# Attention into channel mix on one core: batch 0 loaded in fewer, larger pieces, and each later batch's loads held behind the crossbar transpose of the batch ahead

## The chip, the cores and the metric

The kernel runs on one NeuronCore of a Trainium2 chip. The metric is device time in microseconds (us), from start to end of one execution; the median of several executions counts. The engines are TensorE (PE; its weight loads are listed as PEld), VectorE (DVE), ScalarE (ACT), GpSimd (POOL) and SyncE (SP). Each engine takes its instructions in the order of its own list. POOL and SP issue the transfers here, and 16 DMA engines move the data.

## The reference

Two stages, for 8 batches of 576 tokens with 8 heads of 64:

```python
kv  = einsum('bhsd,bhse->bhde', k, v)          # 64x64 for each batch and head
o   = einsum('bhsd,bhde->bhse', q, kv)
x   = o / sqrt(mean(o*o, -1) + 1e-6) * g_norm  # heads side by side: (8, 576, 512)
xp  = x shifted by one token, zero in front
xk  = mu_k*x + (1-mu_k)*xp;   xr = mu_r*x + (1-mu_r)*xp
kk  = relu(xk @ w_k)                           # w_k 512x1024
out = sigmoid(xr @ w_r) * ((kk*kk) @ w_v)      # w_r 512x512, w_v 1024x512
```

q, k, v, the weights and the output are float32 in memory; the kernel turns inputs into bfloat16 while it loads them.

## The kernel before

**Attention, by batch.** `load(b, n, h0, h1)` (L253) has POOL issue one transfer that brings heads h0 to h1 of q, k or v of batch b, 96 tokens of 6 consecutive positions on 96 partitions. Batch 0 comes in twelve transfers of two heads, batch 1 in six of four, batches 2 to 7 in three of eight heads each (`whole`, L305). The tags k, v and q have two buffers each, so a load of batch b+2 must also wait until batch b's buffer has been read. For a batch: `kv` (L496) multiplies k and v on PE, `kvc` copies the result out; q is turned so that head_dim lies on partitions; `u` (L575) multiplies the turned q, `qT`, with kv; `uc` copies that out, `sq` squares it, `ss` (L597) sums the squares by a matmul with a block of ones, `rr` takes the reciprocal root on ACT, `mul` scales, `d` takes the difference to the token before, and `xk`, `xr` blend.

**How q is turned.** Batches 0 to 2 turn q on PE with an identity (`qtr`, L356 and L553) and copy it out of PSUM (`qc`). Batches 3 to 7 (`BY_DMA`) first regroup the loaded q into a buffer q2 by copies on DVE or ACT (`ql`, L517), and then SP issues one transposing transfer from q2 to qT (`qt`, L531). q2 has one buffer, qT two.

**The gate.** After `qt` of batch b, for b = 3, 4, 5, POOL copies one element of qT (`gate`, L538). POOL cannot run that copy before the transpose has landed, so all that stands behind it in POOL's list is held; the loads of batch b+2 are declared to stand behind it.

**Channel mix, by groups of 512 tokens.** `mix(g)` for nine groups: `k{g}.0` to `.7` (L689, 8 times 4 matmuls of 512 columns), `relu` on ACT, `ksq` (square) on DVE, `r{g}.0` to `.3` (L741, 16 matmuls) with `sig` on ACT, `v{g}.c.p` (L763, 32 matmuls), `out` (product with the sigmoid, on DVE) and `store` on SP. Group 0's k part is cut into `k0.a` (L452, by head pair) and `k0.b` (L709). Both halves of w_k are first multiplied by g_norm on DVE (`g.w_k0`, `g.w_k1`, L289).

**What sets the order.** A table of tokens, `ORDER` (L15 to L63): `Planner.run` goes through it and emits the pieces as they stand there, so it sets the order within each engine's list; the part behind a colon picks the engine, `#2` is the second piece of that name, and `idle:n` puts n matmuls on zeros (L659) into PE's list. Waits between engines are added by the framework from the tiles that are read and written.

Of the kernel before, what the change touches and what calls it, by code (L numbers as in the profile page):

```python
# [15 lines left out]
setup table loadq0.2 loadq0.4 loadv0.4 ident idle:23 qtr0.2 small qtr0.1 loadk0.4 qc0.1#2:DVE loadk0.6 loadq0.6
qc0.1:ACT qc0.2:ACT idle:2 kv0.2 kvc0.2#2:DVE kvc0.2:DVE idle:4 u0.2 loadv0.6 uc0.2:DVE qc0.2#2:ACT sq0.2 idle:3
qtr0.3 qc0.3:DVE idle:4 kv0.3 kvc0.3:ACT kvc0.3#2:ACT qc0.3#2:DVE edge ident9 idle:6 u0.3 u0.2#2 uc0.3:DVE sq0.3
loadv0.0 ss0.2 loadq0.0 rr0.2 idle:8 ss0.3 rr0.3 uc0.2#2:DVE sq0.2#2 mul0.2 loadk0.2 loadv0.2 idle:7 kv0.1
kvc0.1#2:ACT qtr0.0 loadk0.0 qc0.0#2:DVE idle:2 kv0.0 tr9 kvc0.1:DVE qc0.0:DVE u0.1 kvc0.0#2:DVE d0.2 mul0.3 d0.3  # L20
cols ss0.2#2 kvc0.0:ACT u0.0 uc0.1:ACT mk0.2:DVE uc0.0:ACT mk0.3:ACT idle:7 u0.0#2 rr0.2#2 sq0.1 w_k1 idle:4 ss0.1
xk0.2 xk0.3 sq0.0 mul0.2#2 uc0.0#2:ACT sq0.0#2 g.w_k1 idle:4 ss0.0 idle:16 k0.a1.2 d0.2#2 rr0.0 w_k0 rr0.1 mul0.1
loadq1.4 mul0.0 d0.0 mr0.3:DVE d0.1 g.w_k0 loadq1.0 k0.a1.3 ss0.0#2 idle:19 k0.a0.3 rr0.0#2 mr0.1:DVE k0.a0.2
mk0.1:ACT xk0.1 k0.a0.1 qtr1.2 mk0.0:DVE xr0.3 xk0.0 mul0.0#2 d0.0#2 mk0.1#2:DVE mk0.2#2:ACT mk0.0#2:DVE mk0.3#2:ACT
mr0.0:ACT mr0.1#2:DVE loadk1.0 k0.a1.1 xk0.2#2 qc1.2:ACT xk0.0#2 loadv1.0 k0.a1.0 relu0.01 w_r mr0.2:ACT xr0.2
k0.a0.0 relu0.00 qtr1.0 kv1.0 k0.b0 loadk1.4 kvc1.0:ACT mr0.2#2:ACT mr0.0#2:ACT xr0.0 qc1.0:DVE xr0.1 ksq0.01 u1.01
uc1.01:ACT loadv1.4 relu0.10 k0.b1 relu0.11 mr0.3#2:DVE u1.00 g.w_r:DVE xr0.0#2 xr0.2#2 r0.0 uc1.00:DVE w_v r0.1
sig0.0 ksq0.00 ksq0.11 kv1.2 kvc1.2:DVE sq1.00 u1.10 uc1.10:DVE loadv2.0 u1.11 ksq0.10 r0.2 uc1.11:ACT sq1.11 ss1.00
rr1.00 r0.3 sq1.01 ss1.01 v0.0.0 rr1.01 sig0.1 ss1.11 loadk2.0 rr1.11 v0.0.1 sq1.10 ss1.10 rr1.10 v0.1.0 v0.1.1
loadq2.0 v0.2.0 v0.2.1 v0.3.0 v0.3.1 mul1.0 d1.0 xk1.0 loadq3.0 out0.0 mul1.2 d1.2 kv2.0 kvc2.0:ACT qtr2.0 qc2.0:ACT  # L30
qtr2.2 xk1.2 out0.1 k1.0 k1.1 qc2.2:DVE xr1.0 u2.11 ql3.2:DVE uc2.11:ACT relu1.0 ql3.3:DVE ql3.1:DVE ql3.0:ACT u2.00
uc2.00:DVE sq2.00 k1.2 k1.3 k1.4 loadv3.0 relu1.1 k1.5 ksq1.0 u2.10 loadk3.0 relu1.2 xr1.2 u2.01 ksq1.2 uc2.10:ACT
sq2.10 uc2.01:ACT loadq4.0 sq2.01 store0.0#2 k1.6 k1.7 relu1.3 ksq1.3 ss2.00 rr2.00 r1.0 sq2.11 ss2.01 qt3 rr2.01
loadv4.0 r1.1 ksq1.1 r1.2 r1.3 kv3.0 mul2.0 sig1.0 d2.0 ss2.10 sig1.1 kvc3.0:DVE xk2.0 v1.0.0 store0.0 rr2.10 ss2.11
rr2.11 xr2.0 ql4.2:ACT v1.0.1 ql4.3:ACT v1.1.0 mul2.2 loadk4.0 v1.1.1 out1.0 v1.2.0 ql4.0:ACT ql4.1:DVE u3.11 u3.01
v1.2.1 v1.3.0 uc3.01:ACT d2.2 uc3.11:ACT u3.10 uc3.10:ACT xk2.2 u3.00 uc3.00:ACT v1.3.1 k2.0 k2.1 relu2.0 sq3.10
ss3.10 store0.1#2 gate3 loadq5.0 out1.1 k2.2 rr3.10 sq3.01 k2.3 sq3.11 ss3.11 rr3.11 ss3.01 sq3.00 rr3.01 relu2.1
ksq2.0 k2.4 kv4.0 ss3.00 rr3.00 k2.5 relu2.2 xr2.2 mul3.2 kvc4.0:DVE qt4 u4.10 ql5.1:DVE ql5.0:DVE uc4.10:DVE sq4.10
u4.01 store1.0#2 ksq2.2 mul3.0 k2.6 k2.7 ql5.2:DVE uc4.01:ACT store0.1 ql5.3:ACT relu2.3 ksq2.3 u4.00 uc4.00:ACT
u4.11 r2.0 r2.1 uc4.11:ACT d3.2 loadv5.0 sig2.0 ksq2.1 store1.0 sq4.01 ss4.10 rr4.10 r2.2 r2.3 loadk5.0 d3.0 kv5.0  # L40
xk3.2 kvc5.0:DVE v2.0.0 sq4.00 sq4.11 qt5 xr3.0 v2.0.1 v2.1.0 v2.1.1 xk3.0 out2.0 ss4.00 sig2.1 ss4.01 v2.2.0 rr4.00
rr4.01 store2.0 mul4.0 gate4 loadk6.0 store1.1 v2.2.1 v2.3.0 u5.00 uc5.00:DVE u5.10 v2.3.1 out2.1 xr3.2 k3.0 k3.1
d4.0 relu3.0 uc5.10:ACT ksq3.0 ss4.11 sq5.10 store2.0#2 k3.2 loadq6.0 ql6.0:DVE k3.3 rr4.11 store1.1#2 relu3.1
ksq3.1 k3.4 k3.5 gate5 mul4.2 u5.11 relu3.2 ksq3.2 xk4.0 ql6.2:ACT u5.01 uc5.11:ACT sq5.00 k3.6 k3.7 ql6.1:ACT r3.0
sq5.11 relu3.3 r3.1 uc5.01:DVE loadv6.0 sig3.0 ql6.3:ACT d4.2 ksq3.3 xr4.2 kv6.0 kvc6.0:DVE xr4.0 r3.2 r3.3 loadq7.0
store2.1 ss5.11 v3.0.0 qt6 sq5.01 v3.0.1 v3.1.0 v3.1.1 sig3.1 rr5.11 ss5.01 v3.2.0 v3.2.1 xk4.2 ss5.00 rr5.00 rr5.01
v3.3.0 out3.0 v3.3.1 store3.0#2 k4.0 k4.1 relu4.0 ss5.10 out3.1 ql7.2:ACT store3.1#2 mul5.0 ql7.1:DVE rr5.10 d5.0
xk5.0 xr5.0 k4.2 ksq4.0 store2.1#2 k4.3 relu4.1 k4.4 ql7.0:ACT k4.5 relu4.2 u6.10 ksq4.1 u6.00 store3.0 ksq4.2
ql7.3:ACT uc6.10:ACT qt7 uc6.00:DVE sq6.00 k4.6 k4.7 relu4.3 sq6.10 ksq4.3 r4.0 r4.1 u6.11 uc6.11:DVE u6.01 r4.2
store3.1 r4.3 uc6.01:DVE sig4.0 ss6.10 mul5.2 ss6.00 sig4.1 v4.0.0 v4.0.1 loadk7.0 d5.2 xk5.2 rr6.10 rr6.00 v4.1.0  # L50
# [794 lines left out]
```

## Time and profile before

| | |
|---|---|
| median of 3 runs | 220.46 us (220.01 to 221.04) |
| profiled execution: time | 220.13 us |
| profiled execution: span from first to last instruction | 218.4 us |
| PE busy | 198.6 us (91%) |
| DVE busy | 147.1 us (67%) |
| ACT busy | 127.9 us (59%) |
| POOL busy | 30.3 us (14%) |
| moved by DMA | 29.43 MB, 16.78 MB of it by the transfers that POOL issues (queue q0), nearly all the rest by those of SP (q1) |
| granted PE clock, mean | 0.984 |

Busy time is the sum of an engine's instructions; PE's includes the matmuls on zeros. An engine that is busy a small share of the span can still hold up another one at one place, so the waits and the timeline tell more than the shares. "Releaser" is what an instruction waited for last, as the profile infers it.

### The profile page before, as it was taken

To read this page: it belongs to the slowest core of one execution; us is meant where nothing else is said; L and a number is where in the kernel's file an instruction comes from. 1 tells how busy PE (TensorE), PEld (TensorE's weight loads), DVE (VectorE), ACT (ScalarE), POOL (GpSimd) and SP (SyncE) were. 2 spreads that over 40 slices of the span, in tenths; PEclk is the share of its full clock that TensorE was granted. 3 is DMA by queue.
4 is the path that set the end of the run, shared out by engine and by line. 5 is a ranking of instruction groups with operands and counts; after the bars stand their busy time and mean duration, and the time that the engine had idled before them with its cause. 6 is when DMAs were issued, how large, how long until landed. Compare 5 with 4: busy or idle time off the path is not lost.

```text
span 218.4 us, 4018 instructions
## 1 busy us (share of the span) xinstructions
PE 198.6 (91%) x1596; PEld 104.9 (48%) x1615; DVE 147.1 (67%) x319; ACT 127.9 (59%) x162; POOL 30.3 (14%) x48
## 2 busy tenths in 40 slices
PE   5698999999983982999999999999999999999992
...
DMA  4999999999998999995999537250024005115015
GB/s 66 155 199 203 205 207 203 203 225 203 156 191 158 165 155 258 148 144 110 228 238 201 140 100 156 48 144 3 0 63 133 0 0 164 34 26 138 28 33 159
DMA packets 39271, 29.43 MB, mean 135 GB/s; under 512 B 13516, under 2 KB 34772, under 8 KB 39252
## 3 DMA queue, kind: packets, MB, share of 16 engines
q0 software_dynamic: 21632, 16.78, 51.8%
...
## 4 chain that ended last, share of the span: by engine, by line
PE 62%; DMA 32%; POOL 2%; issue 1%; DVE 0%; DVEq 0%; POOLq 0%
PE mm L689 22%; PE mm L763 20%; DMA qT<-q 14%; DMA q<-in_q_dram 12%; PE mm L741 11%; DMA k<-in_k_dram 5%; PE at L597 2%; PE at L575 2%; PE at L780 2%; PE mm L780 2%; PE at L496 1%; POOL q L255 1%; PE at L553 1%; POOL k L255 1%; POOL w_k L281 0%
## 5 line engine op out<-in xcount | busy, mean ns | idle before, releaser
L689 PE MATMUL mm<-xk,w_k 128*128 128x512 bf16 (+1 forms) x282 | 59.8, 362 | 0.3
L763 PE MATMUL mm<-w_v,sqk 128*128 128x512 bf16 x250 | 59.5, 387 | 0.3
L693 ACT ACTIVATE relu<-mm 128x1024 bf16<-128x1024 f32 x36 | 36.9, 1025 | 35.1 <-PE mm L689 23.5
L689 PEld LDWEIGHTS <-w_k 128*128 128x128 bf16 x288 | 28.0, 99 | 26.7 <-issue 2.8
L763 PEld LDWEIGHTS <-sqk 128*128 128x128 bf16 x256 | 24.9, 99 | 29.1 <-issue 3.2
L741 PE MATMUL mm<-w_r,xr 128*128 128x512 bf16 x137 | 33.4, 379 | 0.4
L696 DVE TENSOR_TENSOR sqk<-relu 128x1024 bf16<-128x1024 bf16 x32 | 21.7, 688 | 15.7 <-ACT relu L693 15.7
L767 DVE TENSOR_TENSOR out<-mm,sig 128x1024 f32<-128x1024 f32 x16 | 19.5, 1221 | 14.8 <-PE mm L763 7.1
L601 ACT ACTIVATE rs<-at,eps 128x576 bf16<-128x576 f32 x28 | 19.9, 739 | 8.0 <-PE at L597 7.2
L190 ACT ACT_TABLE_LOAD x18 | 23.1, 1283 | 1.0 <-PEq L829 0.7
L741 PEld LDWEIGHTS <-xr 128*128 128x128 bf16 x144 | 13.6, 98 | 15.5 <-issue 0.7
L746 ACT ACTIVATE sig<-mm 128x1024 bf16<-128x1024 f32 x18 | 18.3, 1024 | 3.3 <-PE mm L741 3.1
L639 DVE TENSOR_SCALAR md<-d,cols 128x576 bf16<-128x576 bf16 x56 | 18.2, 368 | 0.3
L181 ACT CAST uT<-at 128x576 bf16<-128x576 f32 x18 | 11.0, 640 | 10.0 <-PE at L575 9.9
L575 PE MATMUL at<-qT,kv 64*64 64x288 bf16 x112 | 6.5, 299 | 9.0 <-DMA qT<-q 8.6
L582 DVE TENSOR_TENSOR sq<-uT 128x576 bf16<-128x576 bf16 x28 | 11.9, 452 | 3.5 <-ACT uT L181 3.4
L613 DVE TENSOR_TENSOR xT<-uT,rs 128x1152 bf16<-128x1152 bf16 x14 | 10.5, 753 | 3.2 <-ACT rs L601 3.2
L181 ACT COPY q<-q 96x384 bf16<-96x384 bf16 (+1 forms) x16 | 9.4, 628 | 5.6 <-DMA qT<-q 5.6
L659 PE MATMUL mm<-zero 128*128 128x128 bf16 x109 | 11.0, 260 | 1.1 <-DVE zero L227 1.1
L597 PE MATMUL at<-sq,ones 128*128 128x288 bf16 x56 | 11.0, 287 | 0.1
L642 DVE TENSOR_TENSOR xr<-md,xT 128x1152 bf16<-128x1152 bf16 x14 | 10.6, 759 | 0.5
L642 DVE TENSOR_TENSOR xk<-md,xT 128x1152 bf16<-128x1152 bf16 x14 | 10.6, 759 | 0.5
...
## 6 DMA issues: line engine op xcount, KB each, us to landing
...
v<-in_v_dram POOLq DMA_DIRECT2D x6, 576.0 KB, 16.7
k<-in_k_dram POOLq DMA_DIRECT2D x6, 576.0 KB, 17.1
q<-in_q_dram POOLq DMA_DIRECT2D x6, 576.0 KB, 13.0
...
```

The source lines that it names most:

```text
L181: nc.scalar.copy(out=dst, in_=src)
L190: nc.scalar.preload_act_table_set(name)
L601: nc.scalar.activation(out=get(rs)[:, hs, cs], in_=ps.t[:, :, 0:HS], func=AF.Abs_reciprocal_sqrt, bias=eps, scale=1.0 / HD)
L639: nc.vector.tensor_scalar(out=get(md)[:, hp], in0=d.t[:, hp], scalar1=cols[:, m0 + hp:m0 + hp + 1], scalar2=None, op0=ALU.mult)
L642: nc.vector.tensor_tensor(out=dst[:, hs, c0:c0 + S], in0=md.t[:, hs], in1=xT.t[:, hs, 0:S], op=ALU.add)
L689: nc.tensor.matmul(get(ps)[:, fc % 2, a0:a1], w_k_sb[:, cc, 128 * fc:128 * fc + 128], xk[:, cc, x0:x0 + a1 - a0], start=(cc == 0), stop=(c ...
L693: nc.scalar.activation(out=get(rt), in_=ps.t, func=AF.Relu)
L696: nc.vector.tensor_mul(out=get(sqk)[:, 2 * f2:2 * f2 + 2, :], in0=rt.t, in1=rt.t)
L741: nc.tensor.matmul(get(ps)[:, ci % 2, :], xr[:, cc, n0:n0 + 128], w_r_sb[:, cc, :], start=(cc == 0), stop=(cc == NHP - 1))
L746: nc.scalar.activation(out=get(sg), in_=ps.t, func=AF.Sigmoid)
L763: nc.tensor.matmul(get(ps)[:, ci % 2, :], sqk.t[:, fc, 128 * ci:128 * ci + 128], w_v_sb[:, fc, :], start=(fc == 0), stop=(fc == NFC - 1))
L767: nc.vector.tensor_mul(out=get(ot)[:, xs, :], in0=ps.t[:, xs, :], in1=sg.t[:, xs, :])
```

## The change

The loop that loads batch 0 takes pieces of four, two and two heads instead of four times two: nine transfers instead of twelve. The gate behind the transpose of batch b now holds the loads of batch b+1 instead of b+2, and stands behind the transposes of batches 3 to 6 instead of 3 to 5. So the loads of batch 4 are held for the first time, and those of batches 5 to 7 are held by a transpose that comes one batch later. `ORDER` is a new table: head pair 0 is taken first instead of pair 2, and all pieces up to the end stand in a new order. Two lines stand for the table here.

```diff
 ORDER = """
-setup table loadq0.2 loadq0.4 loadv0.4 ident idle:23 qtr0.2 small qtr0.1 loadk0.4 qc0.1#2:DVE loadk0.6 loadq0.6
+setup table loadk0.0 ident loadq0.0 idle:31 qtr0.0 loadv0.0 ident9 idle:6 kv0.0 loadq0.4 loadv0.4 kv0.1 qc0.0#2:ACT
...
-        p = add({"POOL": 0.64 if b == 0 else 0.76}, fn, bufs=[kvq[(n, b)]], due=due, land=(h1 - h0) * (0.42 if b == 0 else 0.37),
+        p = add({"POOL": 0.64 if b == 0 else 0.76}, fn, bufs=[kvq[(n, b)]], due=due, land=(h1 - h0) * (0.39 if b == 0 else 0.37),
...
-    for hp in range(NHP):
+    for h0, h1 in ((0, 4), (4, 6), (6, 8)):
         for i, n in enumerate(("k", "v", "q")):
-            load(0, n, 2 * hp, 2 * hp + 2, -900 + 10 * hp + i)
+            load(0, n, h0, h1, -900 + 10 * h0 + i)
...
-            if b + 2 < B:
+            if b + 1 < B:
                 gate = add({"POOL": 0.3}, lambda _: nc.gpsimd.tensor_copy(out=turned, in_=qT.t[0:1, 0, 0:1]), deps=[c],
                            bufs=[qT], name=f"gate{b}")
                 for n in ("k", "v", "q"):
-                    whole[(n, b + 2)].deps.append(gate)
+                    whole[(n, b + 1)].deps.append(gate)
```

The numbers 0.39 and 0.42 (`land`) are read by nothing that runs: `Planner.add` drops them.

How the lists move, at three places. First, POOL's list from batch 0's loads to the two halves of w_k; a name such as `q_91` is a tile with its number, `96x2x384` is two heads, `x2` two such instructions in a row, and the waits on DMASW are on an earlier transfer of POOL. Before:

```order
L255 DMA q_91<-in_q_dram 96x2x384 x2
L255 DMA v_94<-in_v_dram 96x2x384
L238 AFFINE_SELECT ident_69<-ident_69 128x128 [waits DVE_49]
L255 DMA k_153<-in_k_dram 96x2x384 x2
L255 DMA q_91<-in_q_dram 96x2x384
L255 DMA v_94<-in_v_dram 96x2x384 x2
L255 DMA q_91<-in_q_dram 96x2x384 [waits DMASW0_49]
L255 DMA k_153<-in_k_dram 96x2x384 [waits DMASW1_49]
L255 DMA v_94<-in_v_dram 96x2x384 [waits DMASW2_49]
L255 DMA k_153<-in_k_dram 96x2x384 [waits DMASW3_49]
L281 DMA w_k_79<-in_moe_w_k_dram 128x4x512 [waits DMASW4_49]
L281 DMA w_k_79<-in_moe_w_k_dram 128x4x512 [waits DMASW5_49]
```

After:

```order
L255 DMA k_91<-in_k_dram 96x4x384
L238 AFFINE_SELECT ident_69<-ident_69 128x128 [waits DVE_49]
L255 DMA q_96<-in_q_dram 96x4x384
L255 DMA v_143<-in_v_dram 96x4x384
L255 DMA q_96<-in_q_dram 96x2x384
L255 DMA v_143<-in_v_dram 96x2x384
L255 DMA k_91<-in_k_dram 96x2x384 x2
L255 DMA v_143<-in_v_dram 96x2x384
L255 DMA q_96<-in_q_dram 96x2x384 [waits DMASW0_49]
L281 DMA w_k_79<-in_moe_w_k_dram 128x4x512 [waits DMASW1_49]
L281 DMA w_k_79<-in_moe_w_k_dram 128x4x512 [waits DMASW2_49]
```

Heads 0 to 3 of k, q and v now come first, in three transfers of four heads; what follows w_k up to the load of q of batch 3 keeps its order.

Second, POOL's list from the last loads of batch 3 on; `turned` is the gate. Before:

```order
L255 DMA v_944<-in_v_dram 96x8x384 [waits DMASW4_49,DMASW2_49,PE_49]
L255 DMA k_959<-in_k_dram 96x8x384 [waits DMASW3_49]
L255 DMA q_975<-in_q_dram 96x8x384 [waits DMASW0_49,PE_49]
L255 DMA v_1009<-in_v_dram 96x8x384 [waits DMASW6_49,DMASW5_49]
L255 DMA k_1125<-in_k_dram 96x8x384 [waits DMASW7_49]
L538 COPY turned_77<-qT_1006 1x1 [waits DMAHW6_49]
L255 DMA q_1201<-in_q_dram 96x8x384 [waits DMASW1_49,DVE_49,Activation_49]
```

After:

```order
L255 DMA v_857<-in_v_dram 96x8x384 [waits DMASW7_49,DMASW1_49,PE_49]
L255 DMA k_937<-in_k_dram 96x8x384 [waits DMASW0_49]
L538 COPY turned_77<-qT_946 1x1 [waits DMAHW0_49]
L255 DMA q_954<-in_q_dram 96x8x384 [waits DMASW5_49,PE_49]
L255 DMA k_1128<-in_k_dram 96x8x384 [waits DMASW4_49,DMASW2_49]
L255 DMA v_1184<-in_v_dram 96x8x384 [waits DMASW3_49]
L538 COPY turned_77<-qT_1202 1x1 [waits DMAHW7_49,Pool_49]
```

The three loads of batch 4, which stood ahead of the first gate, now stand behind it, and a second gate stands between them and the loads of batch 5.

Third, DVE's list around the regrouping of batch 3's q (`q2<-q`), behind group 0's last output. Before:

```order
L767 TENSOR_TENSOR out_890<-mm_750,sig_722 128x1024 [waits PE_49]
L183 COPY qT_860<-at_862 128x1152 [waits PE_49]
L639 TENSOR_SCALAR md_902<-d_771,cols_72 128x576 x2
L642 TENSOR_TENSOR xr_82<-md_902,xT_767 128x2x576 [waits DVE_49]
L183 COPY q2_911<-q_777 96x2x6x64 [waits DMASW1_49]
L183 COPY q2_911<-q_777 96x6x64 x4
L183 CAST uT_913<-at_922 128x2x288 [waits PE_49]
```

After:

```order
L767 TENSOR_TENSOR out_781<-mm_764,sig_723 128x1024 [waits PE_49]
L183 COPY qT_861<-at_832 128x1152 [waits PE_49]
L183 COPY q2_889<-q_711 96x6x64 [waits DMASW6_49]
L183 COPY q2_889<-q_711 96x6x64 x3
L183 COPY q2_889<-q_711 96x2x6x64
L183 CAST uT_909<-at_904 128x2x288 [waits PE_49]
L582 TENSOR_TENSOR sq_911<-uT_909 128x2x288 [waits DVE_49]
L639 TENSOR_SCALAR md_930<-d_747,cols_72 128x576 x2
L642 TENSOR_TENSOR xr_82<-md_930,xT_743 128x2x576 [waits DVE_49]
```

The regrouping, which waits for the load of q of batch 3, moved ahead of the blend `xr`, and the last of its copies (not shown) came behind that blend.

## Rows read from the trace of the kernel before

**Rows 1.** The page's 40 slices of the span: busy tenths of PE and of DMA.
```profile
PE   5698999999983982999999999999999999999992
...
DMA  4999999999998999995999537250024005115015
```
**Rows 2.** Waits of PE from 44 to 140 us: us in total, times, longest.
```profile
PE at L575 <- DMA qT<-q: 8.6, 2, 4.6
```
**Rows 3.** Timeline of PE: start, us, operation, count, idle before and its releaser.
```profile
68.82 0.55 PE L575 MATMUL at<-qT,kv 64*64 64x288 bf16 x8 [4.06 <-DMA qT<-q]
69.30 3.43 PE L763 MATMUL mm<-w_v,sqk 128*128 128x512 bf16 x8
...
73.90 1.89 PE L689 MATMUL mm<-xk,w_k 128*128 128x512 bf16 x7
...
85.77 0.44 PE L575 MATMUL at<-qT,kv 64*64 64x288 bf16 x8 [4.56 <-DMA qT<-q]
86.14 3.54 PE L689 MATMUL mm<-xk,w_k 128*128 128x512 bf16 x8
```
**Rows 4.** Windows: busy PE, PEld, DVE, ACT, POOL, then granted PE clock, DMA share, GB/s.
```profile
69.00:73.00 4.00, 4.00 (x24) 1.19 (x16) 2.37 (x6) 3.33 (x6) 2.43 (x4) 0.57 0.61 86
...
86.00:90.00 4.00, 4.00 (x25) 1.20 (x18) 3.25 (x8) 1.74 (x4) 1.56 (x3) 0.57 0.79 145
```
**Rows 5.** SP's timeline: the first of the five transposes being issued.
```profile
51.49 8.78 SPq L532 DMA_TRANSPOSE qT<-q  x1
```
**Rows 6.** Transposes issued in 51:60, in 115:119 and in 130:134: count, us to landing.
```profile
qT<-q SPq DMA_TRANSPOSE x1, 17.3
...
qT<-q SPq DMA_TRANSPOSE x1, 6.3
...
qT<-q SPq DMA_TRANSPOSE x1, 4.9
```
**Rows 7.** DMA queues in 60:62, then in 132:134: packets, MB, share of 16 engines.
```profile
q0 software_dynamic: 376, 0.28, 90.6%
q1 hardware_dynamic: 373, 0.10, 36.1%
...
q1 hardware_dynamic: 1628, 0.42, 109.9%
```
**Rows 8.** POOL's timeline: loads of batches 3 (two), 4 and 5.
```profile
27.54 0.77 POOL L255 DMA_DIRECT2D q<-in_q_dram  x1 [1.65 <-PE at L553]
...
35.21 0.77 POOL L255 DMA_DIRECT2D k<-in_k_dram  x1
47.37 0.77 POOL L255 DMA_DIRECT2D q<-in_q_dram  x1 [11.39 <-PE at L553]
...
69.36 0.77 POOL L255 DMA_DIRECT2D q<-in_q_dram  x1 [0.36 <-issue]
```
**Rows 9.** Loads issued in 27:28, 35.1:36, 69:70 and 100:100.5: KB, us to landing.
```profile
q<-in_q_dram POOLq DMA_DIRECT2D x1, 576.0 KB, 21.9
...
k<-in_k_dram POOLq DMA_DIRECT2D x1, 576.0 KB, 20.1
...
q<-in_q_dram POOLq DMA_DIRECT2D x1, 576.0 KB, 6.4
...
v<-in_v_dram POOLq DMA_DIRECT2D x1, 576.0 KB, 9.1
```
**Rows 10.** Windows of 5 us at the start, columns as in rows 4.
```profile
5.00:10.00 5.00, 3.39 (x46) 2.24 (x46) 1.13 (x4) 1.08 (x3) 4.66 (x8) 1.00 1.13 145
10.00:15.00 5.00, 4.46 (x53) 3.62 (x54) 2.67 (x10) 1.12 (x4) 4.27 (x7) 1.00 1.26 192
15.00:20.00 5.00, 4.45 (x79) 3.37 (x76) 4.50 (x21) 3.50 (x9) 1.63 (x3) 1.00 1.25 206
```
**Rows 11.** The chain that ended last: start, us, what.
```profile
25.06 20.74 DMA q<-in_q_dram
```
**Rows 12.** Window 90:135, columns as in rows 4.
```profile
90.00:135.00 45.00, 44.79 (x359) 24.35 (x360) 39.45 (x79) 36.09 (x44) 3.25 (x5) 1.00 0.96 169
```

More of the change, by code (lines that the diff above doesn't have):

```diff
@@ L15 @@
 ORDER = """
[L16 to L50, printed above, removed]
@@ L61 @@
-k8.0 k8.1 relu8.0 ksq8.0 k8.2 store7.0#2 k8.3 relu8.1 k8.4 ksq8.1 k8.5 relu8.2 k8.6 k8.7 relu8.3 ksq8.2 r8.0 r8.1
-sig8.0 ksq8.3 r8.2 r8.3 v8.0.0 v8.0.1 out8.0 v8.1.0 v8.1.1 sig8.1 v8.2.0 out8.0#2 v8.2.1 v8.3.0 out8.1 store8.0#2
-v8.3.1 v8.3.0#2 store8.0 v8.3.1#2 store8.1 out8.1#2 store8.1#2 out8.1#3 store8.1#3
+setup table loadk0.0 ident loadq0.0 idle:31 qtr0.0 loadv0.0 ident9 idle:6 kv0.0 loadq0.4 loadv0.4 kv0.1 qc0.0#2:ACT
+kvc0.1:ACT kvc0.1#2:ACT kvc0.0:ACT loadk0.6 loadk0.4 qc0.0:DVE qtr0.1 qc0.1#2:DVE kvc0.0#2:ACT idle:5 u0.0#2
@@ new lines @@
+uc0.0#2:DVE qc0.1:ACT idle:1 u0.1 uc0.1:DVE u0.0 uc0.0:ACT qtr0.2 sq0.1 idle:7 kv0.2 kvc0.2:ACT qc0.2#2:DVE edge
+sq0.0#2 qc0.2:DVE ss0.1 kvc0.2#2:ACT rr0.1 small tr9 sq0.0 idle:5 ss0.0 rr0.0 loadv0.6 kv0.3 cols mul0.1 d0.1
+loadq0.6 kvc0.3#2:DVE qtr0.3 qc0.3:ACT qc0.3#2:DVE kvc0.3:ACT mul0.0 d0.0 ss0.0#2 rr0.0#2 idle:6 u0.3 uc0.3:ACT u0.2
+uc0.2:ACT u0.2#2 uc0.2#2:ACT mul0.0#2 d0.0#2 mr0.1:ACT mr0.0#2:ACT mk0.1:ACT sq0.2 idle:12 ss0.2 rr0.2 w_k1 g.w_k1
+sq0.3 idle:10 ss0.3 sq0.2#2 xk0.1 mk0.0:DVE xk0.0 w_k0 g.w_k0 mul0.2 idle:1 ss0.2#2 rr0.3 mk0.1#2:ACT mul0.3 d0.3
@@ new lines @@
+mk0.3:DVE xk0.3 idle:20 k0.a0.1 rr0.2#2 mul0.2#2 mr0.3:ACT d0.2 mk0.2:DVE k0.a1.1 mk0.0#2:DVE xk0.2 d0.2#2 xk0.0#2
+mk0.3#2:DVE loadq1.4 loadq1.0 mk0.2#2:DVE qtr1.2 qc1.2:ACT k0.a0.0 k0.a0.3 xk0.2#2 qtr1.0 mr0.0:DVE k0.a1.3 k0.a0.2
+loadk1.0 k0.a1.2 loadv1.0 xr0.3 mr0.2#2:DVE k0.a1.0 relu0.00 kv1.0 qc1.0:DVE kvc1.0:ACT u1.00 ksq0.00 u1.01
+mr0.1#2:ACT uc1.00:ACT k0.b0 relu0.01 k0.b1 w_r mr0.2:ACT mr0.3#2:DVE uc1.01:DVE relu0.10 g.w_r:DVE sq1.00 ss1.00
+xr0.0 rr1.00 xr0.0#2 relu0.11 xr0.2#2 xr0.2 xr0.1 r0.0 r0.1 ksq0.01 ksq0.10 loadk1.4 loadv1.4 kv1.2 sig0.0 r0.2 w_v
```

46 lines of the change are left out of this document (36 added, 10 removed).

## The prediction, made before the changed kernel ran

> **What bounds the kernel now.** I read the 40 slices first [rows 1]. PE stands at 8 or 9 tenths from the third slice to the last but one, with two holes: the 13th slice (3 tenths) and the 16th (2). DMA stands at 8 or 9 up to the 22nd slice, but for the 19th (5). So the second half is PE alone, the first is PE and DMA side by side, and the holes must come from DMA. The waits of PE say so: all that PE waits for between 44 and 140 us is qT, the transposed q, twice, 8.6 us [rows 2]. The timeline gives both: `u` of batch 3 starts at 68.82 after 4.06 us idle, `u` of batch 4 at 85.77 after 4.56 us [rows 3]. Behind each stand eight matmuls of 512 columns that take 3.43 and 3.54 us, where eight take 1.89 at 73.90 (seven of them recorded) [rows 3]; the granted clock over these stretches is 0.57 [rows 4], so after four idle microseconds PE ran mostly at 1.2 GHz instead of 2.4. The price of both holes is 4.06 + 1.54 + 4.56 + 1.65 = 11.8 us.
>
> Why is qT late? The transpose of batch 3 is issued at 51.49 [rows 5] and lands 17.3 us later; the last one, which no load runs beside, takes 4.9, and the fourth, beside the end of a load, 6.3 [rows 6]. The queues show the reason: from 60 to 62 us the loads (q0) move 376 packets and the transpose (q1) 373, about one for one, but its packets are small, 0.10 MB against 0.28; without loads q1 moves 1628 packets in two microseconds [rows 7]. What it shares the engines with are the loads of batch 4, issued from 47.37 on, four microseconds ahead of it [rows 8].
>
> **The change part by part.**
>
> **The hold, and u of batch 3.** With the gate in front of batch 4's loads, only batch 3's own run beside its transpose; the last, k, is issued at 35.21 and lands 20.1 later, at 55.3 [rows 8, 9]. I take the transpose as issued near 52.7 (below) and landed after 4.9 to 6.3 us, near 58.5, at worst 59. PE wanted qT at 68.82 - 4.06 = 64.8; the new order puts the first half of `u` four matmuls earlier, and with the shift at the start PE comes there near 63. That leaves 4 us, so the first hole closes.
>
> The Trainium skill, Advanced Engine Details and Errata, section X-Bar Transpose (TRN2), has it that transposing transfers are as fast as ordinary ones; were that so beside loads, this one would have landed long before 64.8, the hole would not exist and the hold would win nothing here. Rows 6 and 7 speak against it, 17.3 us to 4.9, and I go by the rows.
>
> **The held loads.** After a gate POOL took 0.5 us to the next load (68.82 to 69.36), and that q landed after 6.4 us [rows 3, 8, 9]: q of batch 4 lands near 59 + 0.5 + 6.4 = 65.9 at worst, 65 more likely. Its regrouping (`ql4.0`, on ACT) stands just before `k2.0`, which PE reached at 73.90; without the first hole (5.6) and with 0.7 for the other terms that is 67.6. It fits by 2 us. What queues behind that copy if it waits is ACT's whole list, `relu` first. The transpose of batch 4 is then issued near 71 and lands near 77. `u` of batch 4 has moved: it stood inside group 2's `k` and now stands behind its eight `k`, four `r` and two of its `v` blocks, 56 matmuls at 1.89/8, 13 us, and some 2.5 us of attention matmuls behind 67.6, so near 83. It fits by 6 us and the second hole closes. From there one round is: gate, 0.5, q 6.4, regrouping 3, transpose 6 = 16 us, against 20 us of PE work in a round (80 matmuls of 512 columns, 19, and the attention's share). So later rounds gain on PE; the tightest I find is the regrouping of batch 7, with 2 us. The loads that come a batch later than before cost nothing, as PE's work covers them; if the cover goes, PE waits one for one.
>
> **Batch 0 in nine pieces.** Between 5 and 15 us DMA moves 145 and then 192 GB/s, and 206 from 15 on [rows 10]. Running at 206 from 3 us would have moved 2.47 MB by 15 us, and it moved 2.0; that bounds the gain at 2.3 us. The other bound is a loss of 0.7: the first `kv` waits for three transfers of four heads, 0.86 MB, near 8.6 us, where its data were there at 7.9. I take 1.4 us gained: half the issues for the first 0.86 MB, so near the upper end, less the later first `kv`. This reaches the end only if the stream of loads moves as a whole. It does: w_r to q of batch 3 keep their order, and the chain runs through q of batch 2, which lands at 45.8 [rows 11] just as PE comes to it, so both shift together.
>
> **The regrouping of batch 3 ahead of the blend.** DVE now comes to it near 45.8, while q of batch 3 lands at 27.54 + 21.9 = 49.4 [rows 8, 9], with the shift 48.0. So DVE stands 2.2 us, and behind it stand `uc`, the blend `xr` that group 1's `r` waits for, and the squares that its `v` waits for. PE has four `k` blocks and two `u` to do meanwhile. I expect 0.7 us of PE waits in `u`, `r` and `v` together; bounds 0 and 2.2. It also moves the transpose's issue to about 52.7.
>
> **At nothing:** one more gate on POOL, which has nothing else to do; five matmuls on zeros fewer, in stretches that wait for data; the order of stores on SP, where each transpose stands behind outputs that are ready before it. PE's real matmuls are the same. With the holes gone, DVE and ACT must do their work in less time; from 90 to 135 us, where PE never waits, they do 39.5 and 36.1 us in 45 [rows 12], so they can.
>
> **Sum**, against the profiled execution: 220.13 - 11.8 - 1.4 + 0.7 = 207.6; its time is 0.33 below the median of the runs, so the median becomes **208.0 us**.
>
> **The rivals.**
> 1. *Late loads.* If the transpose takes 6.3 and q, with two loads and stores beside it, 9.1, as v did after the last gate [rows 9], q of batch 4 lands at 59 + 0.5 + 9.1 = 68.6, 1 us after ACT comes to it, and batch 7's as late: 2 to 4 us of waits, and 1.6 for each that gets as long as the holes of rows 3: 210 to 215, say 212. For it: little slack at two places. Against it: nothing else competes with a held load. The Trainium skill, DMA: Bandwidth & Descriptors, section Rules for kernel authors, asks to issue a transfer early and wait for it late, which speaks against any hold; this rival is what that would do here, and no row yet shows a held load that PE waits for.
> 2. *The transpose is slow by itself* (slower than before). SP takes 8.78 us to issue the first [rows 5]; if that, and not the loads beside it, made the 17.3, a round is 0.5 + 6.4 + 3 + 17.3 = 27 us against 20 of PE work, all serial now: about 7 us more in each of the four rounds, 28 with the clock's share, in place of 11.8 saved: 235 us. It decides once a lone transpose takes over some 10 us. Against it: 4.9 and 6.3 [rows 6].
> 3. *The start gains nothing*, or DVE's stand costs its 2.2 us: 208.0 + 1.4 + 1.5 = 210.9.
> 4. *The hold does nothing*, since loads were late anyway: the holes stay, 219 to 220. Against it: 47.37 is ahead of 51.49 [rows 5, 8].
>
> **How the numbers follow.** Forecast 0.69, with the time between 205.9 and 210.5: below 208.0 lie the other bound at the start (0.9), no wait for the regrouping (0.7) and the 0.55 us that PE idles from 15 to 20 [rows 10], 205.9 in all. Rival 1 0.15, rival 3 0.10, rival 2 0.05, rival 4 0.01. The range 205.5 to 213 holds the forecast, rival 3 and the lower half of rival 1, about 0.85. One half per cent, 1.1 us, is about what a measurement of this kernel can tell from no change: faster 0.94, same 0.02, slower 0.04.
>
> **What would show it.** Right: transposes of 5 to 7 us each in SP's rows; no wait of PE on qT; granted clock 1.00 from 45 us to the end; w_k landed 1 to 2 us earlier; DVE waiting some 2 us before the first regrouping. Wrong: PE or ACT waiting for the load of q (rival 1); a transpose over 10 us with q0 empty (rival 2); a new wait of PE behind DVE of more than 2 us near 50 to 60 us.

## The result, and the profile after

The changed kernel takes 208.60 us in the median of 4 runs (208.06 to 210.12), the kernel before 220.75 in the same comparison (4 runs): a ratio of 0.946, 95% interval 0.939 to 0.952. A second comparison (6 runs of it) gives 208.73 and 0.947 (0.943 to 0.951). The forecast was 208.0 in a range of 205.5 to 213. The profiled execution takes 208.06 us, with a span of 206.3, against 220.13 before.

The 40 slices of the changed kernel, busy tenths for PE, granted clock in tenths, and DMA:

```profile
PE   6398989999999999999999999999999999999992
PEclk9999999999999999999999999999999999999999
DMA  4999999999989989979996999470052031026224
```

The two holes of [rows 1] are gone: PE stands at 8 or 9 from the third slice to the last but one, and DMA stands at 6 tenths or more up to the 25th slice, where before it fell off after the 22nd. The waits of PE from 20 to 204 us, largest first (line waited on, total, times, longest):

```profile
PE at L780 <- DVE out L787: 0.5, 1, 0.5
PE at L575 <- ACT kv L181: 0.4, 1, 0.4
PE at L496 <- ACT relu L693: 0.3, 1, 0.3
```

No qT is among them, where [rows 2] had 8.6 us of it. The timeline of PE around `u` of batches 3 and 4 (start, us, line, operation, count, idle ahead of it in brackets) shows what answers [rows 3]:

```profile
63.57 0.44 PE L575 MATMUL at<-qT,kv 64*64 64x288 bf16 x8
63.94 3.63 PE L763 MATMUL mm<-w_v,sqk 128*128 128x512 bf16 x16
...
67.87 6.22 PE L689 MATMUL mm<-xk,w_k 128*128 128x512 bf16 x27
...
83.75 0.44 PE L575 MATMUL at<-qT,kv 64*64 64x288 bf16 x8
84.12 1.90 PE L763 MATMUL mm<-w_v,sqk 128*128 128x512 bf16 x8
```

No idle stands ahead of `u`, and behind it sixteen matmuls take 3.63 us, eight 1.90: PE keeps its 2.4 GHz (granted clock 1.00 from 45 to 200 us). Why qT is there in time stands in the rows of SP (issue of the transposes) and of POOL (gate, and the first load behind it):

```profile
53.36 3.80 SPq L532 DMA_TRANSPOSE qT<-q  x1
...
71.57 3.00 SPq L532 DMA_TRANSPOSE qT<-q  x1
```

```profile
59.83 0.18 POOL L538 COPY turned<-qT 1x1 bf16<-1x1 bf16 x1 [24.18 <-DMA qT<-q]
60.34 0.77 POOL L255 DMA_DIRECT2D q<-in_q_dram  x1 [0.34 <-PE at L597]
...
76.55 0.48 POOL L538 COPY turned<-qT 1x1 bf16<-1x1 bf16 x1 [13.90 <-DMA qT<-q]
77.08 0.77 POOL L255 DMA_DIRECT2D q<-in_q_dram  x1
```

The gate runs when the transpose has landed: 6.5 us from issue for batch 3 (17.3 in [rows 6]), 5.0 for batch 4. `u` starts 3.7 and 7.2 us after that. The queues from 54 to 59 us (packets, MB, share of the engines) answer [rows 7]: the loads have all but gone.

```profile
q1 hardware_dynamic: 2379, 0.68, 101.0%
q0 software_dynamic: 65, 0.05, 6.0%
```

The held loads of batch 4 (issues between 60 and 75 us, KB, us to landing), and ACT's copy that q is needed for first:

```profile
q<-in_q_dram POOLq DMA_DIRECT2D x1, 576.0 KB, 6.5
k<-in_k_dram POOLq DMA_DIRECT2D x1, 576.0 KB, 8.7
v<-in_v_dram POOLq DMA_DIRECT2D x1, 576.0 KB, 11.7
```

```profile
68.53 0.83 ACT L181 COPY q<-q 96x768 bf16<-96x768 bf16 x1
```

q lands at 60.34 + 6.5 = 66.8, and ACT comes to the copy at 68.53, without idle that DMA ends: 1.7 us of slack.

The start, by windows (length, busy PE, PEld, DVE, ACT, POOL, clock, DMA share, GB/s), to be laid beside [rows 10]:

```profile
5.00:10.00 5.00, 1.62 (x26) 1.31 (x27) 0.36 (x1) 0.32 (x1) 3.24 (x6) 1.00 1.20 168
10.00:15.00 5.00, 5.00 (x94) 3.81 (x92) 2.79 (x11) 2.79 (x10) 4.62 (x7) 1.00 1.28 201
```

DMA moves 168 and 201 GB/s instead of 145 and 192. The chain before ran through the load of q of batch 2 [rows 11]; how much of the quicker start reaches that place stands in one row of PE, its transposes of that q, before and after:

```profile
45.85 1.21 PE L553 MATMUL at<-ident,q 96*64 96x96 bf16 x48
```

```profile
45.40 1.21 PE L553 MATMUL at<-ident,q 96*64 96x96 bf16 x48 [0.21 <-DMA q<-in_q_dram]
```

That point splits the gain: 0.45 us ahead of it and, from it to the end, 174.28 us before against 162.66 after (the times of the two executions less 45.85 and 45.40), 11.62. The same split is used for the experiments. The first part is not sure: in a second profile of the changed kernel PE came there at 46.06. The second part is the same in that profile, 162.60 us.

### The profile page after: what moved, and what is told of

Read it like the earlier page. It is cut to its first block, busy times and chain, and to the rows that moved or that the text cites. A ratio compares the mean times of both kernels' runs of the same rounds, so it can differ in the third digit from the quotient of the medians.

```text
span 206.3 us, 3984 instructions
## 1 busy us (share of the span) xinstructions
PE 193.7 (94%) x1590; PEld 103.6 (50%) x1610; DVE 145.7 (71%) x319; ACT 125.3 (61%) x160; POOL 28.5 (14%) x46
## 4 chain that ended last, share of the span: by engine, by line
PE 73%; DMA 20%; POOL 2%; issue 2%; DVE 1%; POOLq 0%
PE mm L689 25%; PE mm L763 24%; PE mm L741 13%; DMA q<-in_q_dram 11%; DMA k<-in_k_dram 6%; DMA v<-in_v_dram 3%; PE at L597 3%; PE at L496 2%; PE at L575 2%; PE at L780 2%; PE mm L780 2%; POOL q L255 1%; DVE q L183 0%; DVE out L787 0%; POOL k L255 0%
## 5 line engine op out<-in xcount | busy, mean ns | idle before, releaser
L763 PE MATMUL mm<-w_v,sqk 128*128 128x512 bf16 x248 | 57.9, 379 | 0.6 <-DMA w_v<-in_moe_w_v_dram 0.2
L689 PE MATMUL mm<-xk,w_k 128*128 128x512 bf16 (+1 forms) x283 | 58.2, 355 | 0.3
L763 PEld LDWEIGHTS <-sqk 128*128 128x128 bf16 x256 | 24.2, 98 | 29.2 <-issue 2.0
L741 PE MATMUL mm<-w_r,xr 128*128 128x512 bf16 x137 | 32.9, 379 | 0.6 <-issue 0.2
L181 ACT CAST uT<-at 128x576 bf16<-128x576 f32 x21 | 12.7, 641 | 12.3 <-PE at L575 12.2
L582 DVE TENSOR_TENSOR sq<-uT 128x576 bf16<-128x576 bf16 x28 | 11.8, 452 | 0.2
L538 POOL COPY turned<-qT 1x1 bf16<-1x1 bf16 x4 | 1.1, 263 | 71.8 <-DMA qT<-q 71.8
L625 DVE TENSOR_TENSOR d<-xT 128x1152 bf16<-128x1152 bf16 x14 | 10.6, 757 | 0.5
L659 PE MATMUL mm<-zero 128*128 128x128 bf16 x104 | 9.9, 258 | 1.1 <-DVE zero L227 1.1
L597 PE MATMUL at<-sq,ones 128*128 128x288 bf16 x56 | 10.3, 286 | 0.0
```

The source lines that it names most:

```text
L597: nc.tensor.matmul(get(ps)[:, x, 0:HS], ones, sq.t[:, 2 * gp + x, cs], start=True, stop=True)
L689: nc.tensor.matmul(get(ps)[:, fc % 2, a0:a1], w_k_sb[:, cc, 128 * fc:128 * fc + 128], xk[:, cc, x0:x0 + a1 - a0], start=(cc == 0), stop=(c ...
L741: nc.tensor.matmul(get(ps)[:, ci % 2, :], xr[:, cc, n0:n0 + 128], w_r_sb[:, cc, :], start=(cc == 0), stop=(cc == NHP - 1))
L763: nc.tensor.matmul(get(ps)[:, ci % 2, :], sqk.t[:, fc, 128 * ci:128 * ci + 128], w_v_sb[:, fc, :], start=(fc == 0), stop=(fc == NFC - 1))
```

## The experiments

Two theories at the outset: *the loads make the transpose late, and the hold takes them away* (mine), and *it is the new order of the work that gains, by asking for qT and for the held loads later*. The first two runs take the change apart.

**Old order, new hold.** Before's `ORDER` and its twelve pieces; only the gates and the loads behind them move (one of four places of the table is shown).

```diff
-            if b + 2 < B:
+            if b + 1 < B:
...
-                    whole[(n, b + 2)].deps.append(gate)
+                    whole[(n, b + 1)].deps.append(gate)
...
-kvc4.0:DVE qt4 u4.10 ql5.1:DVE
+kvc4.0:DVE qt4 gate4 loadq5.0 loadv5.0 loadk5.0 u4.10 ql5.1:DVE
```

> The kernel before with its own order of all work and its twelve first pieces; only the hold is changed to one batch ahead. Theory (the loads beside a transpose make it late, so keeping them away closes both holes): every transpose lands 5 to 7 us after its issue, PE never waits on qT, which is worth 11.8 us; but in the old order DVE comes to the regrouping of batch 5 near 75 us while its held q lands near 78.5, and kv of batch 5 comes 2 us early, so 4 to 6 us come back: 213 to 215. Rival (the new order with its later u of batch 4 closes the holes, the hold does little): about 220. Rival (the hold alone is everything): 209.

Measured: 220.10 us (10 runs), ratio 0.999 (0.996 to 1.002). No gain at all, a miss. The transposes are quick (gates 7.2 and 7.1 us after the first two issues) and no wait on qT is left, but PE waits elsewhere. Its largest wait, and the timelines of DVE and PE there:

```profile
PE at L575 <- DVE uT L183: 4.0, 1, 4.0
```

```profile
82.28 0.69 DVE L183 COPY q<-q 96x384 bf16<-96x384 bf16 x3 [5.52 <-DMA q<-in_q_dram]
```

```profile
83.69 0.56 PE L575 MATMUL at<-qT,kv 64*64 64x288 bf16 x8 [3.99 <-DVE uT L183]
84.19 3.42 PE L741 MATMUL mm<-w_r,xr 128*128 128x512 bf16 x8
```

In the old order the regrouping of batch 5 (`ql5`) follows close on the transpose of batch 4. q of batch 5, held until that transpose, lands at 82.2; DVE stands 5.52 us at the copy, the copy of `u` of batch 4 (`uT`) queues behind it, PE waits 3.99 for that, and eight matmuls then run at 1.2 GHz (3.42 us; granted clock 0.50 from 84 to 87 us). This is the wait of rival 1, but not for its reason: q lands 6.6 us after its issue, not 9.1, and it is the old order that asks for it too early. Other waits are 1.6 us at `u` of batch 3 (on `uT` from ACT) and 1.3 (on k).

**New order, old hold.** The changed kernel with the gates holding batch b+2 again and the loads of batch 4 free, issued behind those of batch 3.

```diff
-            if b + 1 < B:
+            if b + 2 < B:
...
-loadk3.0 u2.11 uc2.11:ACT ql3.0:DVE qt3 u2.10 gate3 loadq4.0
+loadk3.0 loadq4.0 loadk4.0 loadv4.0 u2.11 uc2.11:ACT ql3.0:DVE qt3 gate3 u2.10
```

> The changed kernel with the hold of before: the loads of batch 4 stand ahead of the first gate, each gate holds the batch after next. Theory: the transpose of batch 3 shares the engines with three loads again, takes about 17 us from near 53.4 and lands near 70; PE waits 6.5 us at u of batch 3 (63.6) and runs eight matmuls at the lower clock, 1.6 us; u of batch 4 stands late enough in the new order, so only one hole returns: 216 to 217. Rival (the new order did it): 208.6.

Measured: 213.42 us (4 runs), ratio 0.969 (0.966 to 0.973), between the two expectations. PE:

```profile
68.09 0.44 PE L575 MATMUL at<-qT,kv 64*64 64x288 bf16 x8 [2.84 <-DMA qT<-q]
68.46 3.63 PE L763 MATMUL mm<-w_v,sqk 128*128 128x512 bf16 x16
```

The transpose, issued at 54.63 beside three loads, lands after 13.5 us and the first hole is back, but only 2.84 us long and with no slow matmuls behind it. The second hole is not back: the order closes it without the hold, and in two ways. It asks for `u` of batch 4 later (88.27), and it issues the transpose of batch 4 7.5 us behind the first load of batch 5, at 76.09, where before it was 1.9 us; the transpose takes 8.2 us and not 14.5. But this execution came to q of batch 2 at 47.04, 1.6 us later than the changed kernel, so a part of its 213 might not be the hold's. Its granted clock stood at 0.50 and 0.62 from 10 to 15 and 15 to 20 us, where the changed kernel's first profile has 1.00 and its second 0.50 and 0.99. The next run was to remove that.

**New order, old hold, more zeros at the start,** so that PE does not idle ahead of the first q.

```diff
-setup table loadk0.0 ident loadq0.0 idle:31 qtr0.0
+setup table loadk0.0 ident loadq0.0 idle:66 qtr0.0
```

> The new order with the old hold, started with 66 instead of 31 matmuls on zeros, so that PE does not idle ahead of the first q. In the profiled execution of the new order with the old hold PE came to q of batch 2 at 47.0 us, in the changed kernel at 45.4, and the early matmuls were slower there. If those 1.6 us are chance of the start and not the hold's doing, PE comes to q of batch 2 at 45.3 to 45.7 here, the hole of batch 3 (2.84 us) stays, and the time is 211 to 212: the hold is then worth 3 us in the new order. If the old hold itself makes the start late: 47 and 213 to 213.5, and the hold is worth 5.

Measured: 214.56 us (6 runs), ratio 0.975 (0.971 to 0.979), above both expectations. PE came to q of batch 2 at 45.21, and then:

```profile
67.53 0.69 PE L575 MATMUL at<-qT,kv 64*64 64x288 bf16 x8 [4.07 <-DMA qT<-q]
68.16 5.00 PE L763 MATMUL mm<-w_v,sqk 128*128 128x512 bf16 x16
```

PE is at `u` at 63.46, where it was at 65.25 in the run before; the transpose lands at the same time, 67.5 to 68.1. So the earlier start is waited away, and the longer wait lets the clock fall as well (5.00 us for sixteen matmuls instead of 3.63). What the missing hold costs in this execution is thus 4.07 + 1.37 + 0.25 = 5.7 us by the rows, and 6.2 by the split (168.88 from q of batch 2 to the end, against 162.66). In the execution of the run before it is less, 2.84 by the rows and 3.3 by the split (165.96), as its late start lies ahead of that point. The medians, which do not depend on the split, say some 5 to 6.

The four corners: old order with old hold 220.2 to 221.1, old order with new hold 220.1, new order with old hold 213.4 to 214.6, both new 208.6 to 208.7. The hold is worth nothing in the old order and 5 to 6 us in the new one.

**Old order, new hold, the regrouping of batch 5 later.** If one place does the harm, moving it should mend it.

```diff
-u4.10 ql5.1:DVE ql5.0:DVE uc4.10:DVE sq4.10 u4.01 store1.0#2 ksq2.2 mul3.0 k2.6 k2.7 ql5.2:DVE uc4.01:ACT store0.1 ql5.3:ACT relu2.3
+u4.10 uc4.10:DVE sq4.10 u4.01 store1.0#2 ksq2.2 mul3.0 k2.6 k2.7 uc4.01:ACT store0.1 relu2.3
...
-sq4.00 sq4.11 qt5 gate5
+sq4.00 sq4.11 ql5.1:DVE ql5.0:DVE ql5.2:DVE ql5.3:ACT qt5 gate5
```

> Old order with the new hold, and one thing more: the regrouping of batch 5 (four copies, on DVE and ACT) stands behind the copies of u of batch 4 instead of ahead of them. In the old order with the new hold (220.1 us) DVE stood 5.52 us and ACT 3.32 at that regrouping, PE 3.99 behind them, and eight matmuls ran at 1.2 GHz after it (3.42 us where eight take 1.89). If the place of the regrouping on its engines is why the hold gained nothing there, PE's wait of 3.99 and the slow matmuls go, about 5.5 us: 214 to 216. If the old order is bound in some other way, so that the wait only reappears elsewhere: 219 to 220.5.

Measured: 224.82 us (5 runs), ratio 1.019 (1.015 to 1.024): 1.9% more than before, a miss for both expectations. The wait of 3.99 is gone, but:

```profile
91.44 2.86 SPq L532 DMA_TRANSPOSE qT<-q  x1
```

```profile
88.27 0.95 PE L496 MATMUL at<-v,k 96*64 96x64 bf16 x48 [2.67 <-DMA k<-in_k_dram]
...
113.65 1.50 PE L496 MATMUL at<-v,k 96*64 96x64 bf16 x48 [5.42 <-ACT q L181]
```

The transpose of batch 5 is issued at 91.44 instead of 85.99, so the loads of batch 6 follow at 97.0 instead of 93.2, and the regrouping of batch 6, left where it was, stops DVE for 4.15 us and ACT for 2.04; PE loses 5.42 us there, 2.67 waiting for k of batch 5, and 2.7 at `u` of batch 3, where it was 1.6. With the hold, transpose, load, regrouping and next transpose hang on each other from batch to batch, and in the old order moving this one link only moved the wait on. Which of the new order's other moves are needed was not taken apart further, so what in that order makes room for the hold is shown for no single move.

**New order, regrouping of batch 4 earlier.** The reverse, in the changed kernel.

```diff
-uc3.00:ACT v1.2.1 v1.3.0 uc3.01:ACT v1.3.1 out1.0 out1.1 u3.10 u3.11 uc3.11:ACT ql4.0:ACT k2.0
+ql4.0:ACT uc3.00:ACT v1.2.1 v1.3.0 uc3.01:ACT v1.3.1 out1.0 out1.1 u3.10 u3.11 uc3.11:ACT k2.0
```

> The changed kernel with one copy moved: the first regrouping copy of batch 4 stands ahead of ACT's copy of u of batch 3, not behind it. ACT comes there near 64 and q of batch 4 lands at 66.8, so ACT stands 2.9 us and the copies of u come 3.7 us later; PE then waits 2 to 4 us for u and, if the wait gets as long as 4 us, pays 1.5 more in matmuls at 1.2 GHz: 210.5 to 213. If the place of the regrouping does not matter and the hold's gain comes from something else in the new order: 208.6, as the changed kernel.

Measured: 208.57 us (4 runs), ratio 0.946 (0.942 to 0.950): no loss, a miss for the theory, though ACT did stand as it had it. ACT, then PE:

```profile
66.09 0.83 ACT L181 COPY q<-q 96x768 bf16<-96x768 bf16 x1 [3.49 <-DMA q<-in_q_dram]
```

```profile
64.08 3.63 PE L763 MATMUL mm<-w_v,sqk 128*128 128x512 bf16 x16
67.64 0.72 PE L575 MATMUL at<-qT,kv 64*64 64x288 bf16 x8
68.29 1.04 PE L689 MATMUL mm<-xk,w_k 128*128 128x512 bf16 x3
```

ACT stands 3.49 us, and PE does not wait, because sixteen `v` matmuls lie between the two halves of `u`: PE needs the copies behind it only at 67.64. Here, as in the run with the old order, an engine that stands at a held load costs what PE has to wait for behind it, not the time it stands.

**One and two loads let through.** v of batch 4 alone, then k and v, ahead of the first gate, to see what loads beside a transpose do to it. The edit for v; for both, "kq" is "q" and loadk4.0 moves too.

```diff
-                for n in ("k", "v", "q"):
+                for n in ("k", "v", "q") if b > 3 else "kq":
...
-loadk3.0 u2.11
+loadk3.0 loadv4.0 u2.11
```

> The changed kernel, but v of batch 4 stands ahead of the first gate, so one load of 0.59 MB runs into the transpose of batch 3. Theory (one packet of the load for one of the transpose while both run): 768 packets of the load hold back as many of the transpose's 2304 for about 4 us, so it takes 7 to 9 us instead of 6.5 and lands near 61 to 62, before PE comes at 63.6: no wait of PE on qT, time unchanged, 208.0 to 209.3. Rival (the length is the transpose's own): 6.5 us as now, same time. Rival (any load beside it makes it as long as all three): 17 us, 216.

> The same with k and v of batch 4 ahead of the first gate: two loads. Theory: 1536 packets held back one for one take about 8 us, the other 768 one more, so the transpose takes 10 to 12 us and lands near 64; PE waits 0 to 1 us for it, the held q lands near 70.5, two microseconds after ACT comes to its regrouping: 209.5 to 211.5. Rival (own length): 208.6. Rival (any load): 216.

Measured: 208.39 us (4 runs; 0.945, 0.940 to 0.949) and 210.10 (4 runs; 0.951, 0.948 to 0.953), as expected. The issue of the transpose and the gate behind it, first with one load let through, then with two, and there PE as well:

```profile
53.39 5.54 SPq L532 DMA_TRANSPOSE qT<-q  x1
```

```profile
61.58 0.18 POOL L538 COPY turned<-qT 1x1 bf16<-1x1 bf16 x1 [14.66 <-DMA qT<-q]
```

```profile
53.09 7.03 SPq L532 DMA_TRANSPOSE qT<-q  x1
```

```profile
64.73 0.20 POOL L538 COPY turned<-qT 1x1 bf16<-1x1 bf16 x1 [17.18 <-DMA qT<-q]
```

```profile
64.73 0.44 PE L575 MATMUL at<-qT,kv 64*64 64x288 bf16 x8 [0.99 <-DMA qT<-q]
```

The transpose of batch 3, issued at 53.4, 53.4 and 53.1, takes 6.5 us beside none of batch 4's loads, 8.2 beside one, 11.6 beside two; beside three it took 13.5 and 14.4 in the new order with the old hold, and 17.3 in the kernel before, where the first of them was issued 4.1 us ahead of it instead of 5.9 and 6.5. SP's issue of it grows with that: 3.8, 5.5, 7.0, then 7.9 and 7.5 us. So the long issue of 8.78 in [rows 5] is an effect of the loads. But it may be a part of how they delay the transpose: from no load to one, landing and issue both grow by 1.7 us, and only from two loads on does the landing grow by more. How much is the issue and how much the packets taking turns [rows 7] these runs do not part. The Trainium skill, Advanced Engine Details and Errata, section X-Bar Transpose (TRN2), has transposing transfers as fast as ordinary ones. A transpose beside none of the next batch's loads agrees: 5.0 to 6.5 us in the changed kernel, where a held load of q, a tile of the same size, takes 6.1 to 8.2. Beside loads, 8.2 to 17.3, the sentence does not carry over.

**A longer hold.** The gate reads uT, the first copy of `u`, instead of qT, and the tokens of the gates and held loads move behind that copy; the loads of batch 4 come some 6 us later, those of later batches more.

```diff
-                gate = add({"POOL": 0.3}, lambda _: nc.gpsimd.tensor_copy(out=turned, in_=qT.t[0:1, 0, 0:1]), deps=[c],
-                           bufs=[qT], name=f"gate{b}")
+                gate = add({"POOL": 0.3}, lambda _: nc.gpsimd.tensor_copy(out=turned, in_=uT.t[0:1, 0, 0:1]), deps=[c],
+                           bufs=[uT], name=f"gate{b}")
```

> The changed kernel with each gate moved from the landed transpose to the first copied-out u of that batch, so each held load starts 4 to 8 us later; the cost of a late load by itself. Theory: the four q land near 71, 92, 108.5 and 130, that is 3, 5, 3.5 and 3 us after ACT comes to their regrouping at 68.5, 87.4, 105 and 127; ACT stands and PE loses most of it, with 1.6 us for each wait that gets long: 216 to 221. Rival (the buffers between the engines take it up, loads have slack of over 5 us): 208.6 to 210.

Measured: 215.34, 218.71, 219.04 and 219.18 us, too far apart for a median with an interval; the lowest lies just under the range expected, the others in it, and all are far above the changed kernel. The profile is of the run at 218.71; what parts it from the one at 215.34 is not shown. ACT and PE:

```profile
72.99 0.83 ACT L181 COPY q<-q 96x768 bf16<-96x768 bf16 x1 [2.80 <-DMA q<-in_q_dram]
```

```profile
74.79 2.75 PE L689 MATMUL mm<-xk,w_k 128*128 128x512 bf16 x12 [1.73 <-ACT relu L693]
...
97.34 0.41 PE L597 MATMUL at<-sq,ones 128*128 128x288 bf16 x2 [3.44 <-ACT rs L601]
```

The load of q is issued at 66.72 instead of 60.34, ACT stands 2.80 at the regrouping, `relu` queues behind it, and PE waits; a batch later it is `rs` and 3.44 us. The later loads also run beside the next transposes again (SP issues those of batches 4 and 5 in 5.14 and 6.54 us), but PE has no wait on qT. The Trainium skill, DMA: Bandwidth & Descriptors, section Rules for kernel authors, asks to issue a transfer early and to wait for it late. This run agrees with it, and so do the waits of the old order with the new hold; the change goes against it and gains, as its own order leaves the 1.7 us of slack that this run takes away.

**Pieces of batch 0.** Twelve pieces of two heads, and six of four, in the changed kernel.

```diff
-    for h0, h1 in ((0, 4), (4, 6), (6, 8)):
+    for h0, h1 in ((0, 2), (2, 4), (4, 6), (6, 8)):
```

```diff
-    for h0, h1 in ((0, 4), (4, 6), (6, 8)):
+    for h0, h1 in ((0, 4), (4, 8)):
```

> The changed kernel with batch 0 in twelve pieces of two heads, in the same order of heads. Theory from the two traces (the pieces moved the load of q of batch 2 by only 0.45 us, and nothing else of the start reaches the end): 208.6 + 0.3 to 0.6, about 209.0. The prediction's term (1.4 us): 210.0. If the pieces matter through PE's first work too: over 210.

> The changed kernel with batch 0 in six pieces of four heads. If fewer issues are what speeds the first loads, w_k lands another 0.3 to 0.5 us earlier and the time is about 208.2; if the first three pieces already gave all there is, 208.6; if the later first data of heads 4 to 7 count, 209 or more.

Measured: 208.96 us (6 runs; 0.949, 0.946 to 0.952) and 209.67 (6 runs; 0.951, 0.948 to 0.955). PE came to q of batch 2 at 45.61 and 47.23. Twelve pieces came out as the theory from the traces had it (209.0), not by the prediction's term (210.0). All intervals overlap that of the changed kernel: between the medians of nine and twelve pieces lie 0.2 to 0.4 us, too little to be told from nothing, and whether six are worse is not settled. One window of the start does tell them apart. The run with twelve:

```profile
10.00:15.00 5.00, 4.54 (x65) 3.32 (x64) 2.71 (x9) 1.79 (x6) 4.03 (x7) 0.51 1.25 192
```

That is the 192 GB/s of [rows 10]; all four profiles with twelve pieces move 192 to 194 from 10 to 15 us, all others 200 to 204. From 5 to 10 us the two groups overlap (145 to 168 and 152 to 173). Six to twelve GB/s over 5 us are 0.03 to 0.06 MB, or 0.15 to 0.3 us at 203 GB/s, an estimate from these rows.

**More zeros in the changed kernel,** with the changed kernel beside it.

```diff
-setup table loadk0.0 ident loadq0.0 idle:31 qtr0.0
+setup table loadk0.0 ident loadq0.0 idle:66 qtr0.0
```

> The changed kernel with 66 instead of 31 matmuls on zeros ahead of the first q, so that PE works through the 3.8 us (4.5 to 8.4) in which it idled. If that idle is why PE runs its first real work at the half clock (0.50 from 10 to 15 us in some executions) and why times spread from 208.1 to 210.1: granted clock 1.00 through the first 20 us, the first key projection at about 20.9 or earlier in every profile, median 207.8 to 208.4, highest below 209.3. If the start is bound by the loads alone: 208.6, and the same spread.

> The changed kernel as it is, beside the one with more zeros on the same chip: 208.6 us, from 208 to 210. In an execution that profiles the first matmuls at half clock, the first key projection starts near 23; in one that profiles full clock, near 21.

Measured: 208.59 (6 runs, 207.92 to 209.60) and 208.73 (6 runs, 207.94 to 209.83), no difference, a miss; what came true is the other reading, a start bound by the loads alone. PE's first rows, with the zeros and then without:

```profile
1.06 5.80 PE L659 MATMUL mm<-zero 128*128 128x128 bf16 x66 [1.06 <-DVE zero L227]
8.38 0.45 PE L356 MATMUL a<-ident,q 96*64 96x96 bf16 x12 [1.52 <-DMA q<-in_q_dram]
```

```profile
1.06 3.49 PE L659 MATMUL mm<-zero 128*128 128x128 bf16 x31 [1.06 <-DVE zero L227]
8.27 0.69 PE L356 MATMUL a<-ident,q 96*64 96x96 bf16 x12 [3.73 <-DMA q<-in_q_dram]
```

The first transposes do run faster (0.45 us for twelve instead of 0.69; granted clock 1.00 from 10 to 15 us instead of 0.50), and PE comes to q of batch 2 at 45.30 instead of 46.06, but neither the median nor the spread of 1.7 to 1.9 us moves. Where that spread lies can be read from the profiles: in the changed kernel and its variants that cost PE no wait, the way from q of batch 2 to the end takes 162.6 to 162.7 us in six profiles (45.30 to 46.06 at that point) and 163.1 in the one with six pieces (47.23). So what differs between these executions stands ahead of that point, and here a later start is paid nearly one for one. What makes the start late in some stays open. No version that was run beats the changed kernel by more than the intervals.

## Why the prediction was right, step by step

**What bounded the kernel** was read rightly: the holes, the slow matmuls behind them and the loads beside the transpose. They were priced at 11.8 us [rows 3, 4]; from q of batch 2 to the end the kernel gained 11.62.

**The transpose.** Predicted alone in 4.9 to 6.3 us, landing at 58.5 to 59, `u` near 63 with 4 us to spare; measured 6.5, 59.8, 63.57 and 3.7, so "at worst 59" was missed by 0.8. The later transposes took 5.0, 5.2 and 5.4. That the loads beside it make it late, and that it is not slow by itself (rival 2), is shown by the ladder 6.5, 8.2, 11.6, 13.5.

**The held loads.** Predicted: q of batch 4 lands at 65 to 65.9, needed at 67.6, 2 us to spare; `u` of batch 4 near 83, 6 to spare. Measured 66.8, 68.5, 1.7; 83.75 and 7.2. The landing broke its bound of 65.9, and ACT came 0.9 later as well, so the slack was kept in part by chance. The tightest later place was not the regrouping of batch 7 (2.2 us) but that of batch 6 (1.2: q landed at 103.8, ACT came at 104.98).

**Credit for the second hole** was given to hold and order together. The new order closes it with the old hold too. By the medians the order alone is worth some 6 to 7 us and the hold, on top of it, 5 to 6; by the split of one execution it is 5.4 (174.28 against 168.88) and 6.2. The prediction did not see that the hold alone is worth nothing in the old order.

**The rival of late loads** was priced by slack at two places and taken to cost PE one for one. It did not happen in the changed kernel, and it took the whole gain in the old order. Two things were missing in the step: that the order is what decides it, which the regrouping's place in before's table could have told; and that a standing engine costs only what PE needs behind it (3.49 us of ACT cost nothing, 5.52 of DVE cost PE 3.99 and the clock).

**The start** was mis-sized: 1.4 us predicted, 0.45 measured at q of batch 2, and not even that is sure (46.06 in the second profile). The sign "w_k landed 1 to 2 us earlier" failed: its halves landed at 17.5 and 20.1 instead of 18.0 and 20.4. The rate rose to 168 GB/s between 5 and 10 us in the first profile, but to 152 in the second, where twelve pieces in the new order have 162; only the next window, 201 against 192, is the pieces'. The estimate leaned on the upper bound, and the choice of value was the error; the bounds (a loss of 0.7, a gain of 2.3) held.

**The regrouping ahead of the blend** was taken at 0.7 us of PE. DVE stood 1.29 us, not 2.2, and PE has no wait from it that the profile lists above 0.4:

```profile
49.02 1.03 DVE L183 COPY q<-q 96x384 bf16<-96x384 bf16 x5 [1.29 <-DMA q<-in_q_dram]
```

**The sum** was 207.6 for the profiled execution and came out 208.06. That it is so near is in part luck, as two mis-sized terms cancel for the most part: 0.95 us too much gain at the start, and 0.5 too little from q of batch 2 to the end (11.1 expected, 11.62 measured), most of which DVE's stand that cost PE next to nothing would account for. At nothing stood right: POOL, SP and DVE's and ACT's load cost PE nothing; at the very end PE now waits 0.5 us for an output of DVE (L787).
